# Moving x's turned 32 x 32 squares through memory instead of 16 DMAs a batch

## The chip, the cores and the metric

The kernel runs on one core of a Trainium2 chip. What counts is the device time of one execution in microseconds. TensorE does the products, VectorE (DVE) and ScalarE (ACT) the element-wise work, GpSimd (POOL) the gathers of rows by index and some element-wise work; SyncE (SP) issues every other DMA. Each engine works through its own instructions in order and waits on semaphores.

## The reference, cut to what matters

A gated linear attention makes x, a mixture of experts sends each token to 2 of 8 experts, and a bilinear layer ends it.

```
state = alpha[t][:, None] * state + outer(k[t], v[t]);  y[t] = q[t] @ state    # 4 x 8 heads, 768 steps, 48 wide
x = y as 3072 tokens x 384 features
noisy = x @ w_gate + log1p(exp(x @ w_noise)) * noise;  top2, softmax over the two
out[mask] += weight * (relu(x[mask] @ w1[e]) @ w2[e])                          # w1: 384 x 1024, w2: 1024 x 384
result = ((x @ w_a) * (x @ w_b)) @ w_out                                       # on the experts' output; 384 x 1536
```

All is float32. The kernel splits each operand of a product into a high and a low part of TensorE's fast float32 kind and adds three products (`prod3`, L785 to L787).

## The kernel before, in words

**Stages.** The first 151 us hold the attention and the router. Then come the experts 0 to 7, up to 832 rows each, and from about 641 us the third stage: six blocks of 512 tokens, each in twelve steps (one per 128 of the 1536 hidden features), an up unit (L1100) and a down unit (L1119) per step. An expert has eight up units (`up_unit`, two halves of 384 rows), a tail of up to 64 more rows that runs in a branch, and six down units (`down_unit`, 128 rows each, 24 products) with a down tail.

**How x gets its layout.** A product contracts over features, so the gathered rows (128 tokens x 384 features) have to be turned: features onto partitions, in three groups `k` of 128. For expert 0, expert 1 and the first block of the third stage TensorE transposes them (`transposed`, L485). For experts 2 to 7, and the other five blocks, DVE turns each 32 x 32 square in place (`blocks`, L504), which leaves the squares in the wrong partitions of `tb`; then `turn` (L506) moves them: for each of 4 x 4 partition pairs one DMA from `tb` to `raw`, in runs of 32 floats, for a batch of up to four row tiles. `parted` (L515) copies a piece of `raw` as the high part on ACT (L517) and takes the low part on DVE (L518). An expert's seven tiles make two batches, of four tiles and of three.

**Order.** The order of instructions is written out by hand. While expert e multiplies, expert e+1 is prepared: its rows are gathered in up units 0 to 6 (L477), turned two units later; the first batch is moved after up unit 6 (L1051), the second after the tail's products (L1059), both by SP. Before down unit j, piece j of the next x is split (L1061). After a down unit ACT evicts the bank into an output tile `o` (L876; the pool `outs` has 3 buffers) and SP stores it to `y2` (L877). Down units use two PSUM banks in turn, so unit j+2 needs the eviction of unit j.

SP also loads the experts' weights (`w_load`, L113, into 6 staging tiles), split by ACT and POOL (L108, L109); and it feeds `decode` (L928): the third stage's weights come as 64-bit numbers, 36 chunks of 384 KB (`wd`, L931), are turned into float32 by ACT (L937, L938, L945), DVE (L939, L942, L943, L949) and POOL (L946, L947), and stored to memory again (`w3f`, L950). `bg` moves a chunk one step per up or down unit; a chunk's first work on ACT stands two `bg` calls behind the issue of its DMA.

In the third stage the next block's x is gathered from `y2` in steps 1 to 4, summed and turned in steps 3 to 6, moved in step 7 (L1142) and split, a tile each, in steps 9 to 12 (L1144).

Of the kernel before, what the change touches and what calls it, by code (L numbers as in the profile page):

```python
# [7 lines left out]
F32 = mybir.dt.float32  # L8
# [13 lines left out]
DM = H * D  # L22
KD = DM // 128
E = 8
# [32 lines left out]
def moe_kernel(ctx: ExitStack, tc, qka, afirst, v, wgn, noise, w1, w2, w3, out):  # L57
# [15 lines left out]
    total = base_of(E - 1) + CAP  # L73
    early = base_of(E - 1) + CAPL
    y2 = tc.dram_tile([total, DM], F32, name="y2")
    wide = w3.dtype != F32
    w3f = tc.dram_tile([128, 3 * NF2 * 384], F32, name="w3f") if wide else None

# [402 lines left out]
    def transposed(t, m, h, l, pt=None):  # L481

        pt = pt or trbank()
        for k in range(KD):
            nc.tensor.transpose(pt[:, k * 128:k * 128 + m], t[:m, k * 128:k * 128 + 128], ident[:m, :m])  # L485
        ptv = pt[:, :DM].rearrange("p (k n) -> p k n", k=KD)[:, :, :m]
        nc.scalar.activation(h, ptv, AF.Copy)
        nc.vector.tensor_tensor(l, ptv, h.bitcast(F32), op=ALU.subtract)
# [5 lines left out]


    flips = {}

    def blocks(key, j, t, m):

        b = j // 4  # L500
        if j % 4 == 0:
            flips[key, b] = tl(tp, [128, 12, 128], F32, "tb", bufs=2)
        tb = flips[key, b][:, 3 * (j % 4):3 * (j % 4) + 3]
        nc.vector.transpose(tb[:m].rearrange("p k n -> p (k n)"), t[:m])  # L504

    def turn(key, b, raw, sizes):  # L506

        tb = flips.pop((key, b))
        for ti in range(4):
            n = 3 * sum(m > 32 * ti for m in sizes)  # L510
            for c in range(4):
                nc.sync.dma_start(raw[32 * c:32 * c + 32, 12 * b:12 * b + n, 32 * ti:32 * ti + 32],  # L512
                                  tb[32 * ti:32 * ti + 32, :n, 32 * c:32 * c + 32])

    def parted(src, h, l):  # L515
# [4 lines left out]
    raws_of = {}  # L520
    sizes = [min(128, CAP - 128 * j) for j in range(NJ)]

    def x_blocks(e, j):
        blocks(e, j, gat.pop((e, j)), sizes[j])

    def x_turn(e, b):
        if b == 0:
            raws_of[e] = tl(tp, [128, 3 * NJ, 128], F32, "raw")
        turn(e, b, raws_of[e], sizes[4 * b:4 * b + 4])

    def x_part(e, j):
        s = slice(128 * j, 128 * j + sizes[j])
        parted(raws_of[e][:, 3 * j:3 * j + 3, :sizes[j]], Xh[:, :, s], Xl[:, :, s])

    def routing(s):
        yield from choose(s)
# [240 lines left out]
    HB = tl(hpool, [128, 2 * NF1 * ROWS], F32R, "HB")  # L777
    Hh = HB[:, :NF1 * ROWS].rearrange("p (f n) -> p f n", f=NF1)
    Hl = HB[:, NF1 * ROWS:].rearrange("p (f n) -> p f n", f=NF1)
    outs = sctx.enter_context(tc.tile_pool(name="outs", bufs=3))  # L780

    def prod3(ps, a, b, first, last):

# [206 lines left out]
    def x2_blocks(i):  # L990
        blocks("x2", i % TB, x2r.pop(i)[1], 128)

    def x2_turn():
        raws_of["x2"] = tl(tp, [128, 3 * NJ, 128], F32, "raw")
        turn("x2", 0, raws_of["x2"], [128] * TB)

    def x2_part(i):
        j = i % TB
        parted(raws_of["x2"][:, 3 * j:3 * j + 3], *x2_at(i))


    more_rows = {}
# [36 lines left out]
    for e in range(1, E - 1):  # L1039
        for f in range(NF1):  # L1040
            up_unit(e, f, [(0, MAIN // 2), (MAIN // 2, MAIN // 2)])
            if f == 2:
                load_more_rows(e)
            if e == 2 and f == 5:
                over = nc.values_load(flag[0:1, 0:1], min_val=0, max_val=1)
            if f < NJ:
                gather(e + 1, f)
            if f >= 2:
                x_blocks(e + 1, f - 2)
            if f == 6:  # L1050
                x_turn(e + 1, 0)  # L1051
            w_split()
            w_load()
            bg()
        tail = up_tail(e)
        next(tail)
        bg()
        x_blocks(e + 1, 6)
        x_turn(e + 1, 1)  # L1059
        for j in range(NJ):  # L1060
            x_part(e + 1, j)  # L1061
            if j < NJ - 1:
# [82 lines left out]

    for u in range(NB * NF2):
        blk, f = divmod(u, NF2)
# [13 lines left out]
    with tc.tile_pool(name="over", bufs=1) as op:  # L1161
# [10 lines left out]
        with tc.If(over > 0):  # L1172
# [11 lines left out]
            def flip(dst, src):  # L1184
                pt = bank(0)
                for k in range(KD):
                    ks = slice(k * 128, k * 128 + 128)
                    nc.tensor.transpose(pt[:, ks], src[:, ks], ident)
# [86 lines left out]
```

## Time and profile before

| | us |
|---|---|
| median of the timed runs (lowest, highest) | 1103.93 (1101.8, 1105.57) |
| the profiled execution's own time | 1101.91 |
| its span, first to last instruction | 1100.1 |
| TensorE busy | 1036.3 (94%) |
| VectorE, ScalarE, GpSimd busy | 510.7, 416.7, 414.3 |
| mean granted clock of TensorE | 0.973 |

Busy time says how long an engine had an instruction in work. A wait is the idle time of an engine just before an instruction, put down to whatever released it. The chain of work that ended last is followed back from the end, at each step to what released it. The granted clock is TensorE's, as a share of 2.4 GHz. SP's instructions, which issue DMAs, are its queue's (SPq) and not counted as busy.

### The profile page before, as it was taken

The page shows a single profiled execution, that of the slowest core. Times are in us where ns is not written, and L with a number is a line of the kernel's source. Part 1 is how long each engine was busy: PE and PEld are TensorE (multiplying, and loading weights), DVE is VectorE, ACT ScalarE, POOL GpSimd, SP SyncE. Part 2 cuts the span into 40 slices and gives each one's busy share as a digit, 9 for nine tenths or more (in the row PEclk, how much of TensorE's full clock was granted, in tenths as well). Part 3 has the DMA queues.
Part 4 walks back from the last instruction along what each step waited for, and adds up shares of the span by engine and source line. Part 5 has one row for each costly group of instructions (what it writes and reads, how often), then busy time and mean ns, then how long its engine had stood idle before and what let it go on. Part 6 is the DMA issues. An engine that isn't in the chain of part 4 may idle for free.

```text
span 1100.1 us, 18122 instructions
## 1 busy us (share of the span) xinstructions
PE 1036.3 (94%) x6868; PEld 953.2 (87%) x6868; DVE 510.7 (46%) x940; ACT 416.7 (38%) x913; POOL 414.3 (38%) x446
## 2 busy tenths in 40 slices
PE   7998879999989999979989899999999999999997
PEld 5887779999989989879979888888888888888886
DVE  8998575663725545545534335323233232232221
ACT  2554322644526455434444424322222222222222
POOL 5688414573827465655744532411020020000000
PEclk9999779999999999998999999999999999999998
DMA  8776114556556666655663633313012021010000
GB/s 326 262 287 234 40 35 134 157 155 176 171 116 203 128 221 141 208 147 165 177 174 100 193 112 73 101 51 65 18 53 46 29 64 24 29 26 4 29 1 31
DMA packets 154511, 129.47 MB, mean 118 GB/s; under 512 B 102832, under 2 KB 138416, under 8 KB 154416
## 3 DMA queue, kind: packets, MB, share of 16 engines
q1 hardware_dynamic: 147888, 108.54, 34.0%
q0 software_dynamic: 6528, 19.67, 6.1%
q8 instruction: 58, 0.95, 0.4%
q14 instruction: 37, 0.30, 0.1%
HBM read 89.83 MB, written 26.74 MB: 106 GB/s over the span
## 4 chain that ended last, share of the span: by engine, by line
PE 65%; SPq 9%; DVE 8%; DMA 5%; POOL 3%; issue 3%; ACT 2%; ACTq 0%; DVEq 0%; POOLq 0%
PE bank L786 20%; PE bank L787 20%; PE bank L785 20%; SPq L512 8%; DMA wd<-w 3%; DMA y<-o 2%; DVE pm L641 1%; POOL W L109 1%; DVE D L606 1%; DVE A L610 1%; POOL row L477 1%; SPq L113 1%; PE bank L652 1%; PE bank L636 1%; DMA wst<-w3f 1%
## 5 line engine op out<-in xcount | busy, mean ns | idle before, releaser
L109 POOL TENSOR_TENSOR W<-wst,W 128x384 fp32r<-128x384 f32 x136 | 143.3, 1058 | 169.9 <-ACT W L108 168.3
L785 PE MATMUL bank<-W,HB 128*128 128x384 f32 x528 | 182.2, 345 | 18.6 <-ACT o L876 18.6
L787 PE MATMUL bank<-W,HB 128*128 128x384 f32 x528 | 179.4, 340 | 0.0
L786 PE MATMUL bank<-W,HB 128*128 128x384 f32 x528 | 179.2, 339 | 0.0
L785 PE MATMUL bank<-X,W 128*128 128x384 f32 (+1 forms) x483 | 170.7, 353 | 5.7 <-ACT X L517 5.7
L786 PE MATMUL bank<-X,W 128*128 128x384 f32 (+1 forms) x483 | 170.1, 352 | 0.3 <-DVE X L518 0.2
L1112 DVE TENSOR_TENSOR p<-bank,a 128x512 f32<-128x512 f32 x72 | 49.8, 692 | 258.9 <-PE bank L787 254.8
L787 PE MATMUL bank<-X,W 128*128 128x384 f32 (+1 forms) x483 | 169.9, 352 | 0.0
L785 PEld LDWEIGHTS bank<-W,HB 128*128 128x128 f32 x528 | 101.0, 191 | 23.7 <-ACT o L876 21.8
L972 POOL DMA_INDIRECT row<-y,row x48 | 46.6, 970 | 188.5 <-DVE row L980 172.0
L1114 ACT ACTIVATE HB<-p 128x512 fp32r<-128x512 f32 x72 | 45.5, 632 | 155.8 <-DVE p L1112 153.6
L1110 ACT ACTIVATE a<-bank 128x512 f32<-128x512 f32 x72 | 43.0, 597 | 160.7 <-PE bank L787 160.7
L786 PEld LDWEIGHTS bank<-W,HB 128*128 128x128 f32 x528 | 101.0, 191 | 1.7
L785 PEld LDWEIGHTS bank<-X,W 128*128 128x128 f32 x483 | 92.9, 192 | 10.2 <-ACT X L517 6.3
L787 PEld LDWEIGHTS bank<-W,HB 128*128 128x128 f32 x528 | 100.9, 191 | 0.0
L786 PEld LDWEIGHTS bank<-X,W 128*128 128x128 f32 x483 | 92.9, 192 | 4.7 <-DVE X L518 0.8
L803 DVE SCALAR_TENSOR_TENSOR HB<-bank,HB 128x384 fp32r<-128x384 f32 x128 | 69.3, 553 | 57.8 <-ACT HB L802 50.2
L787 PEld LDWEIGHTS bank<-X,W 128*128 128x128 f32 x483 | 92.7, 192 | 3.9
L802 ACT ACTIVATE HB<-bank 128x384 fp32r<-128x384 f32 x128 | 62.0, 490 | 82.0 <-PE bank L787 76.3
L477 POOL DMA_INDIRECT row<-xd,idx x56 | 60.5, 1081 | 39.9 <-DVE idx L386 23.2
L108 ACT ACTIVATE W<-wst 128x384 fp32r<-128x384 f32 x144 | 72.9, 519 | 2.8 <-DMA wst<-w3f 2.4
L1115 DVE TENSOR_TENSOR HB<-p,HB 128x512 fp32r<-128x512 f32 x72 | 49.9, 692 | 50.3 <-ACT HB L1114 48.9
(262 smaller groups left out, 1946.5 us busy)
## 6 DMA issues: line engine op xcount, KB each, us to landing
wst<-w SPq DMA_DIRECT2D x128, 192.0 KB
ring<-qka SPq DMA_DIRECT2D x22, 768.0 KB
wd<-w SPq DMA_DIRECT2D x36, 384.0 KB
y<-o SPq DMA_DIRECT2D x48, 192.0 KB
raw<-tb SPq DMA_DIRECT2D x176, 48.0 KB
w3f<-u SPq DMA_DIRECT2D x36, 192.0 KB
wst<-w3f SPq DMA_DIRECT2D x36, 192.0 KB
v<-v SPq DMA_DIRECT2D x12, 384.0 KB
```

The source lines that it names most:

```text
L108: nc.scalar.activation(h, raw, AF.Copy)
L109: eng.tensor_tensor(l, raw, h.bitcast(F32), op=ALU.subtract)
L477: nc.gpsimd.indirect_dma_start(out=t[:m], out_offset=None, in_=xd[:SPLIT * 128] if a else xd, in_offset=bass.IndirectOffsetOnAxis(ap=ix, a ...
L512: nc.sync.dma_start(raw[32 * c:32 * c + 32, 12 * b:12 * b + n, 32 * ti:32 * ti + 32], tb[32 * ti:32 * ti + 32, :n, 32 * c:32 * c + 32])
L785: nc.tensor.matmul(ps, ah, bh, start=first, stop=False)
L786: nc.tensor.matmul(ps, ah, bl, start=False, stop=False)
L787: nc.tensor.matmul(ps, al, bh, start=False, stop=last)
L802: nc.scalar.activation(Hh[:, f, s], pu, AF.Relu)
L803: nc.vector.scalar_tensor_tensor(Hl[:, f, s], pu, 0.0, Hh[:, f, s].bitcast(F32), op0=ALU.max, op1=ALU.subtract)
L972: nc.gpsimd.indirect_dma_start(out=t, out_offset=None, in_=src, in_offset=bass.IndirectOffsetOnAxis(ap=row[:, i, k:k + 1], axis=0))
L1112: nc.vector.tensor_tensor(p, ps[1], a, op=ALU.mult)
L1115: nc.vector.tensor_tensor(l, p, h.bitcast(F32), op=ALU.subtract)
```

## The change

The squares go through a scratch tensor `xt` in memory: one DMA (two for the second batch) writes `tb` out row by row, four read it back, each for 32 partitions and in runs of 96 floats. For that, DVE's turning reads every third feature and writes the three groups side by side, and feature 3r + k now lies in group k; TensorE's transposes read with the same step, and the host lays out the rows of `w1`, `w_a` and `w_b` to match. In the expert stages the reading back stands one unit behind the writing out (up unit 7; before down unit 1), in the third stage one step behind (step 8). The third stage splits two tiles each in steps 10 and 11. The pool `outs` gets a fourth buffer.

```diff
+    xt = tc.dram_tile([ROWS, DM], F32, name="xt")
-            nc.tensor.transpose(pt[:, k * 128:k * 128 + m], t[:m, k * 128:k * 128 + 128], ident[:m, :m])
+            nc.tensor.transpose(pt[:, k * 128:k * 128 + m], t[:m, k::KD], ident[:m, :m])
...
-        nc.vector.transpose(tb[:m].rearrange("p k n -> p (k n)"), t[:m])
+        nc.vector.transpose(tb[:m].rearrange("p (c k n) -> p c k n", c=4, k=KD),
+                            t[:m].rearrange("p (c r k) -> p c k r", c=4, k=KD))
-    def turn(key, b, raw, sizes):
+    def turn_out(key, b, rows):
         tb = flips.pop((key, b))
-        for ti in range(4):
-            n = 3 * sum(m > 32 * ti for m in sizes)
-            for c in range(4):
-                nc.sync.dma_start(raw[32 * c:32 * c + 32, 12 * b:12 * b + n, 32 * ti:32 * ti + 32],
-                                  tb[32 * ti:32 * ti + 32, :n, 32 * c:32 * c + 32])
+        n, m = divmod(rows, 128)
+        d = xt[512 * b:512 * b + 128 * n].rearrange("(j p) d -> p j d", p=128)
+        nc.sync.dma_start(d, tb[:, :n])
+        if m:
+            nc.sync.dma_start(xt[512 * b + 128 * n:512 * b + rows], tb[:m, n])
+    def turn_in(raw, b, rows):
+        for c in range(4):
+            nc.sync.dma_start(raw[32 * c:32 * c + 32, 16 * b:16 * b + rows // 32],
+                              xt[512 * b:512 * b + rows, 96 * c:96 * c + 96].rearrange("(n r) w -> r n w", r=32))
-    def parted(src, h, l):
+    def parted(raw, m, h, l):
+        src = raw[:, :m // 32].rearrange("p t (k n) -> p k t n", k=KD)
+        h, l = (x.rearrange("p k (t n) -> p k t n", n=32) for x in (h, l))
...
-    outs = sctx.enter_context(tc.tile_pool(name="outs", bufs=3))
+    outs = sctx.enter_context(tc.tile_pool(name="outs", bufs=4))
...
             if f == 6:
-                x_turn(e + 1, 0)
+                x_out(e + 1, 0)
+            if f == 7:
+                x_in(e + 1, 0)
...
-        x_turn(e + 1, 1)
         for j in range(NJ):
+            if j == 0:
+                x_out(e + 1, 1)
+            if j == 1:
+                x_in(e + 1, 1)
             x_part(e + 1, j)
...
         if f == 6:
-            x2_turn()
-        if f >= 12 - TB:
-            x2_part(i + f - 12 + TB)
+            turn_out("x2", 0, BLK)
+        if f == 7:
+            new_raw("x2")
+            turn_in(raws_of["x2"], 0, BLK)
+        if f in (9, 10):
+            for j in range(2):
+                x2_part(i + 2 * (f - 9) + j)
```

## Rows read from the trace of the kernel before

**Rows 1.** The page, chain that ended last: shares of the span by line.

```profile
PE bank L786 20%; PE bank L787 20%; PE bank L785 20%; SPq L512 8%; DMA wd<-w 3%; DMA y<-o 2%; DVE pm L641 1%; POOL W L109 1%; DVE D L606 1%; DVE A L610 1%; POOL row L477 1%; SPq L113 1%; PE bank L652 1%; PE bank L636 1%; DMA wst<-w3f 1%
```

**Rows 2.** Waits of TensorE: who, for whom, us in total, times, longest.

```profile
PE bank L785 <- ACT o L876: 18.6, 10, 5.9
...
PE bank L785 <- ACT X L517: 5.7, 2, 3.7
...
PE bank L858 <- ACT o L876: 2.4, 1, 2.4
```

**Rows 3.** Timeline of SP: start, us, line, DMA, count.

```profile
296.70 11.60 SPq L512 DMA_DIRECT2D raw<-tb  x16
...
309.00 0.43 SPq L931 DMA_DIRECT2D wd<-w  x1
```

**Rows 4.** Timeline of ACT; in brackets the idle time before and its end.

```profile
313.27 0.56 ACT L937 ACTIVATE ah<-wd 128x384 f32<-128x384 f32 x1 [9.36 <-DMA wd<-w]
...
374.76 0.52 ACT L517 ACTIVATE X<-raw 128x384 fp32r<-128x384 f32 x1 [7.01 <-DMA raw<-tb]
```

**Rows 5.** Windows at half clock: us, busy by engine, PEclk, DMA share, GB/s.

```profile
633.77:637.18 3.41, 3.41 (x14) 3.31 (x14) 0.78 (x2) 1.24 (x3) 0.00 (x0) 0.50 0.00 1
sum 22.94, PE 22.94 PEld 22.84 DVE 15.35 ACT 14.72 POOL 16.74; mean PE 3.82 PEld 3.81 DVE 2.56 ACT 2.45 POOL 2.79
```

**Rows 6.** Timeline of TensorE, inside a half-clock stretch and outside one.

```profile
317.16 0.52 PE L785 MATMUL bank<-W,HB 128*128 128x384 f32 x1
317.48 0.52 PE L786 MATMUL bank<-W,HB 128*128 128x384 f32 x1
...
372.79 0.33 PE L785 MATMUL bank<-W,HB 128*128 128x384 f32 x1
...
373.66 0.34 PE L787 MATMUL bank<-W,HB 128*128 128x384 f32 x1
```

**Rows 7.** Line 512: duration of an issue in ns, min/median/max, first and last start.

```profile
L512 SPq DMA_DIRECT2D raw<-tb x272: 585/618/1939, 234.0 to 989.5; - x136
```

**Rows 8.** The chain in order of time: pieces that are a y DMA.

```profile
385.56 2.04 DMA y<-o
...
507.10 3.46 DMA y<-o
...
566.05 7.23 DMA y<-o
```

**Rows 9.** DMA packets, MB, share: 752 to 764 us (L512), 1091 to 1098 (outputs).

```profile
q1 hardware_dynamic: 6000, 0.74, 43.0%
...
q1 hardware_dynamic: 576, 0.79, 30.9%
```

**Rows 10.** Timelines of SP and TensorE: first L512, first down product, two experts.

```profile
234.04 11.23 SPq L512 DMA_DIRECT2D raw<-tb  x16
...
242.08 0.33 PE L785 MATMUL bank<-W,HB 128*128 128x384 f32 x1
...
476.64 4.58 SPq L512 DMA_DIRECT2D raw<-tb  x5
...
480.08 0.34 PE L785 MATMUL bank<-W,HB 128*128 128x384 f32 x1
```

**Rows 11.** Timeline of ACT, the last eviction.

```profile
1094.49 0.49 ACT L1129 ACTIVATE o<-bank 128x384 f32<-128x384 f32 x1 [1.93 <-DMA out<-o]
```

**Rows 12.** Timeline of TensorE, first products of a block of the third stage.

```profile
713.43 0.49 PE L785 MATMUL bank<-HB,EX 128*128 128x512 f32 x1
...
714.53 0.40 PE L787 MATMUL bank<-HB,EX 128*128 128x512 f32 x1
...
715.46 0.39 PE L785 MATMUL bank<-HB,EX 128*128 128x512 f32 x1
```

**Rows 13.** Groups by line and shape, DVE: busy us, mean ns, idle before.

```profile
L504 DVE STREAM_TRANSPOSE tb<-row 128x384 f32<-128x384 f32 x56 | 32.1, 572 | 3.4 <-DMA row<-xd,idx 2.5
```

**Rows 14.** Line 485, weight load: ns min/median/max, first and last start, forms.

```profile
L485 PEld LDWEIGHTS bank<-ident,row x54: 136/141/231, 141.9 to 635.8; 128*128 128x128 f32 x48, 64*128 64x128 f32 x6
```

More of the change, by code (lines that the diff above doesn't have):

```diff
@@ L496, in moe_kernel @@
     flips = {}
+    raws_of = {}
+    sizes = [min(128, CAP - 128 * j) for j in range(NJ)]
     def blocks(key, j, t, m):
-        b = j // 4
         if j % 4 == 0:
-            flips[key, b] = tl(tp, [128, 12, 128], F32, "tb", bufs=2)
-        tb = flips[key, b][:, 3 * (j % 4):3 * (j % 4) + 3]
-        nc.vector.transpose(tb[:m].rearrange("p k n -> p (k n)"), t[:m])
-    def turn(key, b, raw, sizes):
-        tb = flips.pop((key, b))
-        for ti in range(4):
-            n = 3 * sum(m > 32 * ti for m in sizes)
-            for c in range(4):
-                nc.sync.dma_start(raw[32 * c:32 * c + 32, 12 * b:12 * b + n, 32 * ti:32 * ti + 32],
-                                  tb[32 * ti:32 * ti + 32, :n, 32 * c:32 * c + 32])
@@ L515, in parted @@
-    def parted(src, h, l):
+            flips[key, j // 4] = tl(tp, [128, 4, DM], F32, "tb", bufs=2)
+        tb = flips[key, j // 4][:, j % 4]
+        nc.vector.transpose(tb[:m].rearrange("p (c k n) -> p c k n", c=4, k=KD),
+                            t[:m].rearrange("p (c r k) -> p c k r", c=4, k=KD))
+    def turn_out(key, b, rows):
+        tb = flips.pop((key, b))
+        n, m = divmod(rows, 128)
[3 more added lines that the diff above has]
+            nc.sync.dma_start(xt[512 * b + 128 * n:512 * b + rows], tb[:m, n])
@@ L517, in parted @@
+    def turn_in(raw, b, rows):
[5 more added lines that the diff above has]
+        h, l = (x.rearrange("p k (t n) -> p k t n", n=32) for x in (h, l))
         nc.scalar.activation(h, src, AF.Copy)
         nc.vector.tensor_tensor(l, src, h.bitcast(F32), op=ALU.subtract)
-    raws_of = {}
@@ L521, in moe_kernel, with new_raw, x_out, x_in @@
-    sizes = [min(128, CAP - 128 * j) for j in range(NJ)]
+    def new_raw(key):
+        raws_of[key] = tl(tp, [128, 4 * NJ, 96], F32, "raw")
     def x_blocks(e, j):
         blocks(e, j, gat.pop((e, j)), sizes[j])
-    def x_turn(e, b):
+    def x_out(e, b):
+        turn_out(e, b, sum(sizes[4 * b:4 * b + 4]))
+    def x_in(e, b):
         if b == 0:
-            raws_of[e] = tl(tp, [128, 3 * NJ, 128], F32, "raw")
-        turn(e, b, raws_of[e], sizes[4 * b:4 * b + 4])
+            new_raw(e)
+        turn_in(raws_of[e], b, sum(sizes[4 * b:4 * b + 4]))
@@ L531, in x_part @@
     def x_part(e, j):
         s = slice(128 * j, 128 * j + sizes[j])
-        parted(raws_of[e][:, 3 * j:3 * j + 3, :sizes[j]], Xh[:, :, s], Xl[:, :, s])
+        parted(raws_of[e][:, 4 * j:4 * j + 4], sizes[j], Xh[:, :, s], Xl[:, :, s])
     def routing(s):
@@ L991, in x2_blocks @@
         blocks("x2", i % TB, x2r.pop(i)[1], 128)
-    def x2_turn():
-        raws_of["x2"] = tl(tp, [128, 3 * NJ, 128], F32, "raw")
-        turn("x2", 0, raws_of["x2"], [128] * TB)
     def x2_part(i):
         j = i % TB
-        parted(raws_of["x2"][:, 3 * j:3 * j + 3], *x2_at(i))
+        parted(raws_of["x2"][:, 4 * j:4 * j + 4], 128, *x2_at(i))
     more_rows = {}
@@ L1187, in flip @@
                     ks = slice(k * 128, k * 128 + 128)
-                    nc.tensor.transpose(pt[:, ks], src[:, ks], ident)
+                    nc.tensor.transpose(pt[:, ks], src[:, k::KD], ident)
                 nc.scalar.activation(dst, pt[:, :DM], AF.Copy)
@@ L1257 @@
         "noise": inputs["moe_noise"].reshape(NT, 128, E).transpose(1, 0, 2),
-        "w1": inputs["moe_w1"].reshape(E, KD, 128, NF1, 128).transpose(0, 2, 3, 1, 4).reshape(E, 128, NF1, 384),
+        "w1": inputs["moe_w1"].reshape(E, 128, KD, NF1, 128).transpose(0, 1, 3, 2, 4).reshape(E, 128, NF1, 384),
         "w2": inputs["moe_w2"].reshape(E, NF1, 128, DM).transpose(0, 2, 1, 3),
-        "w3": np.stack([inputs[k].reshape(KD, 128, NF2, 128).transpose(1, 2, 0, 3).reshape(128, NF2, 384)
+        "w3": np.stack([inputs[k].reshape(128, KD, NF2, 128).transpose(0, 2, 1, 3).reshape(128, NF2, 384)
                         for k in ("moe2_w_a", "moe2_w_b")]
```

## Prediction

> **What bounds the kernel now.** I began with the chain that ended last. Three lines of TensorE's products hold 20% of the span each, and behind them stands one that is no arithmetic: SP's queue at L512, 8% [rows 1]. L512 issues the DMAs that move the turned squares of x from `tb` to `raw`. A share of a chain is no loss, because TensorE may work meanwhile, so I read next what TensorE itself waits for. It waits 18.6 + 2.4 us for ACT's eviction `o` (L876) and 5.7 us for ACT's copy of x (L517), 26.7 us together [rows 2].
>
> Why ACT is late stands in the timelines. One batch of turned squares is 16 DMAs and holds SP for 11.60 us; only then does SP issue the encoded third-stage weights (`wd`), at 309.00 [rows 3]. ACT comes to L937 with no weights to read and idles 9.36 us until 313.27; in the next expert, until 374.76, it idles 7.01 us for the squares themselves [rows 4]. All engines run in order, so one late DMA holds every ACT instruction behind it, `o` among them, and TensorE runs out of free banks. Ten of the eleven stalls on `o`, and both on L517, lie between 276 and 580 us, where experts 2 to 6 prepare the next expert's x in this way; one lies in expert 1.
>
> The stalls cost more than their length. Behind the five longest, in which TensorE stood for 2 to 5.9 us, the granted clock is 0.50 for a while, the 1.2 GHz level: six such stretches sum to 22.94 us, of which one of 3.41 us, at 633.77, belongs to another wait (that for L488) [rows 5]; that leaves 19.53 us. There products start 0.32 us apart, against 0.174 us (five steps in 0.87) at full clock [rows 6], so 1 - 0.174/0.32 = 0.46 of it is lost: 8.9 us.
>
> **The change part by part.**
>
> *Fewer issues on SP.* An issue at L512 takes 0.618 us [rows 7], 0.66 us with the pause behind it, 16 of them 10.6 us. The new batch is one write to memory (two for the second batch of an expert, whose last 64 rows go alone) and four reads back. With the 0.66 us of a like-formed issue that is 3.3 to 4.0 us, some 7 us of SP saved per batch, 14 per expert, in just the stretch that makes `wd` and `y` late. If all waits of ACT go, the stalls of 26.7 us and the slow clock behind them, 8.9 us, go with them: 35.6 us.
>
> *The round trip.* The four reads wait on SP until the write has landed. A `y` DMA of 192 KB lands 2.04 to 7.23 us after its issue, 3.46 in a usual case [rows 8]. Four output DMAs (768 KB, all in 1536-byte runs) hold 0.309 x 16 engines x 7 us = 34.6 us of engine time, 2.2 us over 16 engines [rows 9]; one of them 0.54. So the write of 768 KB lands after 3.7 to 8.9 us, 5.1 usual (the `y` figure plus 3 x 0.54). The fourth read is issued 3 x 0.66 = 2.0 us later and lands 2.0 to 7.2 us after that, 3.5 usual. The whole: 7.7 to 18.1 us, and I take 10.6. The data itself is no worse than now: 6000 runs of 128 bytes cost 0.43 x 16 x 12 = 82.6 us of engine time, 13.8 ns each [rows 9], 5.2 us per batch over 16 engines; 2048 runs of 384 bytes lie between the 2.2 us of long runs and those 5.2 us (3.0 by a line between the two sizes), to which the write adds its 2.2.
>
> *What this wait may hold.* The first piece of x is split ahead of the eviction of down unit 0, and TensorE needs that bank when down unit 1 ends. In the tightest expert the squares are ready at 476.64 and the down units start at 480.08 [rows 10]; two units are 48 products of 0.174 = 8.35 us; less 1.0 us for the copy (0.52, [rows 4]) and an eviction of like size, 10.8 us are left. In expert 1 the same sum gives 15.4 us (squares at 234.04, down units from 242.08); the other four lie between. So the usual 10.6 us just fits and I count no stall; at 18.1 us the excess is 2.7 to 7.3 us, a mean of 5, six times 30 us, with six slow stretches of 3.41 x 0.46 = 1.57 us, 39 us in all. Queued on SP behind the wait are a load of expert weights, the next `wd` or `w3f`, the second batch's write and `y` of unit 0. At the usual landing SP stands some 5 us less what passes between the two steps, against 11.6 us now. The second batch is read back after `y` of unit 0 and needed after three more down units, 12.5 us, so it is hidden; uncovered, its excess would fall on ACT at unit 4.
>
> *Fourth output buffer.* In the expert stages it lets `o` run one more unit ahead of a late `y`; its gain is inside the 26.7. At the end ACT idles 1.93 us before the last output because the third-last buffer is still in flight [rows 11]. With four that wait goes and the last DMA leaves 1.9 us sooner: 1.9 us, all on the path. The same waits at other block ends hold no TensorE.
>
> *Third-stage x one step earlier.* Now the fourth piece is split in step 12, and the next block's second product waits for it: the first two products take 1.10 us, from 713.43 to 714.53, where the next four take 0.93, 0.23 each [rows 12]. Steps 10 and 11 with two pieces each end that: 1.10 - 0.47 = 0.63 us at each of five block ends, 3.2 us. Two pieces in a step add 1 us to ACT and to DVE in a step of 6.2 us. The round trip lies in two steps with SP idle.
>
> *Permuted features.* The squares and 54 TensorE transposes now read every third element. No row shows a three-element step, so I bound it: from nothing to doubling. DVE's transpose is 0.572 us [rows 13], off the path; doubled it takes 0.6 us from the 10.8. TensorE's weight load for one is 141 ns [rows 14]; doubled and not hidden, 54 x 0.141 = 7.6 us. A gain is excluded, since the same elements are read. I take nothing, as the count of elements stays, and the rows show nothing else that would set it. The transposes of the overflow branch don't run here.
>
> The Trainium skill ("SBUF — State Buffer", section "Door 1: The DMA port swizzle") speaks against this part: SBUF is read in lines of 16 bytes, and reads that touch a line fewer than twice lose speed; a 12-byte step hits a line 1.3 times. No row here shows it. What it would make of the time is the third rival below.
>
> *Sum.* 35.6 + 1.9 + 3.2 = 40.7 us. I hold back 4 us: 2 for a round trip that is late in one or two experts, 2 for `wd`, which takes 4.3 us from issue (309.00) to ACT's release (313.27) even when SP is free [rows 3, 4]. That leaves 36.7. The profiled execution took 1101.9 us (span 1100.1 plus 1.8 around it), 2.0 below the median of the timed runs, 1103.9; by the median the forecast is 1103.9 - 36.7 = 1067.2, about 1067 us.
>
> **The rivals.**
>
> 1. *Half the stalls stay, because `wd` is the cause and not SP.* For: ACT waits for `wd` in the largest stall [rows 4], and 4.3 us of its delay is the transfer. Against: only 4.3 of the 9.36 us there pass after its issue, the other 5.1 before it. Half of 35.6, 18, stays, of which 2 are held back already: 1067 + 16 = 1083 us.
>
> 2. *Slower.* The wait for the write's landing takes the place of the issues: SP stands at step 7 in each of six experts, with `wd` and `y` behind it, and ACT stands at the first piece of x. It decides where the round trip passes 18 us in the mean expert: there the new stalls (39 us) eat the 40.7 won. At 20 us the excess is 6.9 us on average, six times 41.4 + 9.4 = 50.8, less 40.7: 1104 + 10 = 1114 us. For: the slowest `y` took 7.23 us [rows 8]. Against: it needs that everywhere, and twice in a row.
>
> 3. *The strided reads cost.* TensorE's 54 transposes pay 7.6 us: 1067 + 7.6 = 1075 us, a little more if the DVE delay uncovers the round trip. For: nothing in the trace; against: nothing either.
>
> 4. *The change does nothing where it aims:* another wait stands just behind each stall and only the last stage's 5.1 us come: 1099 us. Against: L512 stands ahead of the late DMA [rows 3].
>
> **How the numbers follow.** Forecast 0.70, rival 1 0.12, rival 3 0.08, rival 2 0.05, rival 4 0.05. All of the first three are faster by over 0.3% (3.3 us, about what a measurement here can tell from no change), and most of rival 4: 0.92 faster, 0.03 no change, 0.05 slower. The forecast's own range is from 1058 (nothing held back, and 5 us more should the stall before 633.77 and its slow stretch go too) to 1076. To leave out no more than 2 in 10 it must reach rival 1, so 1058 to 1086.
>
> **What would show it.** L512's 16 issues per batch gone from SP and the issue of `wd` right behind the write; TensorE's waits for L876 and L517 below 4 us together; granted clock 1.00 between 276 and 580 us except for single stretches; block ends with 0.23 us between the first two products; the last eviction right behind the third. Each reading back within 11 us of the write's issue would show the round trip as sized. It is wrong if ACT idles for `raw` in most experts (round trip too long), if ACT still idles for `wd` by 5 us or more (rival 1), or if TensorE's transposes lie further apart (rival 3).

## The result and the profile after

The changed kernel takes 1064.16 us (median of 4 runs, 1062.98 to 1065.93); the kernel before took 1104.75 us beside it (1101.8 to 1105.68). The ratio is 0.9638, with a 95% interval from 0.9614 to 0.9662: 40.6 us less by the medians, where 36.7 were forecast. The profiled execution of the changed kernel is its slowest run, 1065.93 us (span 1064.2), 36.0 less than that of before; the sums below are made between these two profiled executions. One run further down, 1264.71 us of the kernel with features in order at a granted clock of 0.746, is left out of that kernel's median and ratio.

Most lines have moved by some 14: the products of `prod3` are L799 to L801, ACT's eviction `o` L890, its copy of x L528, the first work on `wd` L951; the write to `xt` is L514 (L516 for 64 rows), the reading back L521.

| stretch, us | before | after | difference |
|---|---|---|---|
| start to the first down product of expert 1 | 242.08 | 244.63 | +2.55 |
| from there to the first down product of expert 7 | 361.89 | 325.13 | -36.76 |
| from there to the first eviction of the last block | 487.03 | 485.70 | -1.33 |
| from there to the end of the span | 9.15 | 8.70 | -0.45 |

The first line is no effect of the change: across the runs of all kernels below that point comes between 240.7 and 244.6 us. What counts most is the second line, the six experts in whose time an x is turned for the next one.

The chain that ended last in the kernel after, shares of the span by line:

```profile
PE bank L799 25%; PE bank L800 25%; PE bank L801 25%; DMA raw<-xt 2%; DVE pm L655 1%; DMA xt<-tb 1%; DVE D L620 1%; DVE A L624 1%; PE bank L650 1%; PE bank L666 1%; PE bank L486 1%; SPq L521 0%; POOL row L986 0%; POOL row L478 0%; POOL W L110 0%
```

Against [rows 1] SP's queue has gone from 8% to nothing, and TensorE's products have grown from 60% to 75%: the chain now runs through arithmetic. `wd` and `y` are not in it any more; the new round trip (`xt<-tb`, `raw<-xt`) is, with 3%.

Waits of TensorE in the kernel after (who, for whom, us in total, times, longest), the two lines that concern the experts and what follows them:

```profile
PE bank L486 <- DVE X L489: 4.6, 1, 4.6
...
PE bank L799 <- ACT o L890: 1.6, 3, 0.6
```

Of the 26.7 us of [rows 2], 1.6 are left on `o` (2.9 in a second profiled execution of the same kernel), and no line for the copy of x is left. The first line is a wait that the change was not about; it was there before and is taken up below.

Windows over the same work, six experts from the first down product of expert 1 to that of expert 7, first of the kernel before and then of the kernel after (window: us, busy by engine, granted clock, DMA share, GB/s):

```profile
242.08:603.97 361.89, 334.88 (x1846) 327.29 (x1844) 178.01 (x300) 170.71 (x386) 204.43 (x192) 0.97 0.60 163
```

```profile
244.63:569.76 325.13, 322.67 (x1845) 318.58 (x1844) 179.18 (x300) 171.70 (x386) 200.95 (x193) 1.00 0.68 202
```

The same count of products, to one record. What TensorE did not work fell from 361.89 - 334.88 = 27.0 us to 2.5, and the time in which it worked fell by 12.2 us, with the granted clock up from 0.97 to 1.00 of 2.4 GHz. 24.5 + 12.2 = 36.7 us is the whole of the second line of the table.

Two more windows of the kernel after, from 276 us up to the fall of the clock during that wait for DVE, and the stretch at half clock:

```profile
276.00:598.70 322.70, 316.97 (x1813) 312.56 (x1812) 179.49 (x293) 171.24 (x385) 205.43 (x197) 1.00 0.68 203
598.73:605.56 6.83, 5.57 (x20) 5.48 (x21) 3.34 (x7) 2.56 (x6) 0.29 (x1) 0.50 0.13 45
```

The six half-clock stretches of [rows 5] are gone but the one behind the wait for DVE, and that one is twice as long as before, 6.83 against 3.41 us. The length is one of this execution: in the second one of the same kernel the stretch is as long as before:

```profile
601.09:604.50 3.41, 3.41 (x14) 3.31 (x13) 1.17 (x3) 1.65 (x5) 0.00 (x0) 0.50 0.00 0
```

SP's timeline in the kernel after, in the same expert as [rows 3] (start, us, line, DMA, count):

```profile
297.55 0.43 SPq L514 DMA_DIRECT2D xt<-tb  x1
...
298.66 0.53 SPq L945 DMA_DIRECT2D wd<-w  x1
302.82 1.92 SPq L521 DMA_DIRECT2D raw<-xt  x4
304.83 0.43 SPq L114 DMA_DIRECT2D wst<-w  x1
305.31 0.43 SPq L964 DMA_DIRECT2D w3f<-u  x1
305.79 0.43 SPq L514 DMA_DIRECT2D xt<-tb  x1
306.32 0.51 SPq L516 DMA_DIRECT2D xt<-tb  x1
```

Where 16 issues held SP for 11.60 us, the write takes 0.43 us, and `wd` leaves 1.1 us behind its start instead of 12.3 us. SP then stands for 3.6 us until the write has landed (a load of weights, `w3f` and the second batch's write are queued behind it) and issues the four reads in 1.92 us.

ACT's timeline in the same stretch (in brackets the idle time before and what ended it):

```profile
304.64 0.56 ACT L951 ACTIVATE ah<-wd 128x384 f32<-128x384 f32 x1
...
310.59 0.53 ACT L528 ACTIVATE X<-raw 128x384 fp32r<-128x384 f32 x1 [4.95 <-DMA raw<-xt]
311.02 0.47 ACT L890 ACTIVATE o<-bank 128x384 f32<-128x384 f32 x1
```

ACT finds `wd` there, without the 9.36 us of [rows 4]. It still idles before x, 4.95 us here, and the eviction stands behind that; but it does so while TensorE has two banks to fill. That the idle time of ACT has not gone and TensorE's has is what its waits for DMAs say:

```profile
ACT X L528 <- DMA raw<-xt: 25.7, 6, 5.8
...
ACT ah L951 <- DMA wd<-w: 6.3, 7, 2.1
```

Before, ACT waited 71.2 us for `wd` (17 times), 21.4 for the squares and 19.5 for `y`; `y` has no line any more.

### The profile page after: what moved, and what is told of

Read it like the earlier page. It is cut to its first block, busy times and chain, and to the rows that moved or that the text cites. A ratio compares the mean times of both kernels' runs of the same rounds, so it can differ in the third digit from the quotient of the medians.

```text
span 1064.2 us, 17897 instructions
## 1 busy us (share of the span) xinstructions
PE 1028.1 (97%) x6868; PEld 950.8 (89%) x6868; DVE 518.3 (49%) x940; ACT 417.9 (39%) x913; POOL 410.9 (39%) x446
## 4 chain that ended last, share of the span: by engine, by line
PE 79%; DVE 6%; DMA 3%; POOL 2%; issue 2%; ACT 1%; SPq 0%; POOLq 0%; ACTq 0%; DVEq 0%
PE bank L799 25%; PE bank L800 25%; PE bank L801 25%; DMA raw<-xt 2%; DVE pm L655 1%; DMA xt<-tb 1%; DVE D L620 1%; DVE A L624 1%; PE bank L650 1%; PE bank L666 1%; PE bank L486 1%; SPq L521 0%; POOL row L986 0%; POOL row L478 0%; POOL W L110 0%
## 5 line engine op out<-in xcount | busy, mean ns | idle before, releaser
L110 POOL TENSOR_TENSOR W<-wst,W 128x384 fp32r<-128x384 f32 x136 | 140.3, 1037 | 138.7 <-ACT W L109 137.1
L799 PE MATMUL bank<-W,HB 128*128 128x384 f32 x528 | 179.9, 341 | 1.6 <-ACT o L890 1.6
L801 PE MATMUL bank<-W,HB 128*128 128x384 f32 x528 | 177.8, 337 | 0.0
L800 PE MATMUL bank<-W,HB 128*128 128x384 f32 x528 | 177.6, 336 | 0.0
L799 PE MATMUL bank<-X,W 128*128 128x384 f32 (+1 forms) x483 | 168.7, 349 | 0.8 <-DVE HB L817 0.8
L800 PE MATMUL bank<-X,W 128*128 128x384 f32 (+1 forms) x483 | 168.1, 348 | 0.0
L801 PE MATMUL bank<-X,W 128*128 128x384 f32 (+1 forms) x483 | 167.9, 348 | 0.0
L799 PEld LDWEIGHTS bank<-W,HB 128*128 128x128 f32 x528 | 100.0, 189 | 4.3 <-ACT o L890 2.6
L800 PEld LDWEIGHTS bank<-W,HB 128*128 128x128 f32 x528 | 99.9, 189 | 1.7
L801 PEld LDWEIGHTS bank<-W,HB 128*128 128x128 f32 x528 | 99.7, 189 | 0.0
L799 PEld LDWEIGHTS bank<-X,W 128*128 128x128 f32 x483 | 91.4, 189 | 5.0 <-DVE HB L817 1.3
L801 PEld LDWEIGHTS bank<-X,W 128*128 128x128 f32 x483 | 91.4, 189 | 3.9
L800 PEld LDWEIGHTS bank<-X,W 128*128 128x128 f32 x483 | 91.4, 189 | 3.9 <-issue 0.3
```

The lines of the kernel that those rows point to most:

```text
L110: eng.tensor_tensor(l, raw, h.bitcast(F32), op=ALU.subtract)
L799: nc.tensor.matmul(ps, ah, bh, start=first, stop=False)
L800: nc.tensor.matmul(ps, ah, bl, start=False, stop=False)
L801: nc.tensor.matmul(ps, al, bh, start=False, stop=last)
```

## The experiments

The theory: SP's queue of 16 issues per batch was the cause, through the DMAs that stood behind it, and the round trip just fits. The rivals: the bytes per run or `wd` by itself; the buffer; the strided reads, as a cost that makes the gain smaller. The first four ran together, against 1102.32 us of the kernel before (11 runs). The changed kernel itself ran in this group only; between groups the ratios to the kernel before are what compares.

**The changed kernel again.**

> The changed kernel itself, as the mark for the three beside it. Theory (SP's issues made the encoded weights and the y stores late, and ACT and TensorE with them): 1062 to 1066 us again, ratio 0.962 to 0.966. No rival says otherwise.

1062.52 us (1060.48 to 1065.5), ratio 0.9629 [0.9607, 0.9652]. What the next three are held against.

**Three output buffers.**

```diff
-    outs = sctx.enter_context(tc.tile_pool(name="outs", bufs=4))
+    outs = sctx.enter_context(tc.tile_pool(name="outs", bufs=3))
```

> The changed kernel with three output buffers again. Theory: with SP free a y store lands about 3.5 us after its issue, so three buffers do in the expert stages; only the end pays, where the last eviction waits 1.9 us again: 1.9 us slower than the changed kernel (range 1 to 4), TensorE's wait for the eviction below 4 us. Rival (the fourth buffer is what cured the stalls): TensorE's wait for the eviction returns to 10 to 20 us and the time goes up by 12 to 25 us.

1063.24 us, 0.9645 [0.9624, 0.9667]: 0.7 us more, and the intervals overlap. In the experts the fourth buffer does nothing: the waits on `o` are 1.4 us (2 times) with three. At the end the wait of [rows 11] is back, as ACT's timeline of this kernel shows:

```profile
1051.36 1.53 ACT L1144 ACTIVATE o<-bank 128x384 f32<-128x384 f32 x3 [1.25 <-PE bank L801]
1054.65 0.49 ACT L1144 ACTIVATE o<-bank 128x384 f32<-128x384 f32 x1 [1.77 <-DMA out<-o]
```

The last eviction starts 3.29 us after the first; with four buffers it is 1.6 us. And yet from the first eviction to the end it is 8.98 us here against 8.70. Of the 1.9 us that I had put on the path, 1.3 still show at the last output's issue, 2.50 us after the first eviction with four buffers and 3.81 with three; they are lost behind it (see the last experiment).

**The third stage's split as before.**

```diff
-        if f in (9, 10):
-            for j in range(2):
-                x2_part(i + 2 * (f - 9) + j)
+        if f >= 12 - TB:
+            x2_part(i + f - 12 + TB)
```

> The changed kernel with the third stage's split back in steps 9 to 12, one tile each. Theory: 0.63 us at each of five block ends, 3.2 us slower than the changed kernel (range 2.5 to 3.8), the first two products of a block taking 1.10 us again. Rival (the first product's wait was hidden by what follows): 0 to 1 us.

1065.61 us, 0.9673 [0.965, 0.9696]: 3.1 us more, as expected (the two intervals just touch, 0.965 and 0.9652). TensorE's timeline at the first products of a block in this kernel, and below it in the kernel after:

```profile
677.64 0.48 PE L799 MATMUL bank<-HB,EX 128*128 128x512 f32 x1
678.41 0.50 PE L800 MATMUL bank<-HB,EX 128*128 128x512 f32 x1 [0.29 <-DVE HB L529]
678.74 0.39 PE L801 MATMUL bank<-HB,EX 128*128 128x512 f32 x1
```

```profile
681.09 0.39 PE L799 MATMUL bank<-HB,EX 128*128 128x512 f32 x1
681.32 0.40 PE L800 MATMUL bank<-HB,EX 128*128 128x512 f32 x1
681.55 0.40 PE L801 MATMUL bank<-HB,EX 128*128 128x512 f32 x1
```

The first two products take 1.10 us, to the hundredth what [rows 12] have, against 0.46. The wait in brackets is 0.29 us; the rest of the loss lies in products that run alone, so that counting idle time only would have given less than half.

**Features in order.** The round trip stays; DVE's turning and TensorE's transposes read adjoining features again, and the host's layouts are those of before.

```diff
-            nc.tensor.transpose(pt[:, k * 128:k * 128 + m], t[:m, k::KD], ident[:m, :m])
+            nc.tensor.transpose(pt[:, k * 128:k * 128 + m], t[:m, k * 128:k * 128 + 128], ident[:m, :m])
...
-                            t[:m].rearrange("p (c r k) -> p c k r", c=4, k=KD))
+                            t[:m].rearrange("p (k c r) -> p c k r", c=4, k=KD))
...
```

> The changed kernel without the permuted features: group k is again features 128k to 128k+127, the transposes on TensorE read contiguous columns, and DVE reads its squares as runs of 32 floats in another order, so that the squares still leave as 96-float runs. The changed kernel's trace shows a TensorE weight load of 202 ns for a transpose where the kernel before has 141, and 696 ns for a DVE transpose where it has 572. Theory (the three-element step costs what these rows say): back to 141 and 572 ns, and 54 x 0.061 = 3.3 us faster at most, range 1.5 to 3.5, nearly all before 250 us. Rival (the weight loads are covered, and the later start of the experts is chance): within 1 us of the changed kernel.

1062.28 us (5 runs), 0.9635 [0.9612, 0.9659]. No difference to the kernel with the stride that the times can show (0.2 us, with intervals of some 2.5 us to either side), though the instructions themselves differ. TensorE's weight loads of the transposes (ns min/median/max), strided in the kernel after and then in order:

```profile
L486 PEld LDWEIGHTS bank<-ident,row x54: 185/202/283, 144.5 to 602.8; 128*128 128x128 f32 x48, 64*128 64x128 f32 x6
```

```profile
L486 PEld LDWEIGHTS bank<-ident,row x54: 135/141/230, 142.2 to 601.2; 128*128 128x128 f32 x48, 64*128 64x128 f32 x6
```

And DVE's turning of squares (busy us, mean ns of one, idle before), in the same order:

```profile
L506 DVE STREAM_TRANSPOSE tb<-row 128x384 f32<-128x384 f32 x56 | 39.0, 696 | 4.9 <-DMA row<-xd,idx 4.1
```

```profile
L506 DVE STREAM_TRANSPOSE tb<-row 128x384 f32<-128x384 f32 x56 | 32.1, 573 | 4.7 <-DMA row<-xd,idx 3.9
```

The stride costs 61 ns per weight load (43%) and 123 ns per turning (21%). In order they are as in [rows 13, 14]. 54 x 0.061 = 3.3 us of weight loading and 6.9 us of DVE lie beside other work, for all that the times show. The rule of the Trainium skill that I had weighed ("SBUF — State Buffer", section "Door 1: The DMA port swizzle") agrees with these rows in its direction: reads at a 12-byte step are slower. What it would have made of this kernel's time, the third rival, did not come.

The next four ran together, against 1101.64 us of the kernel before (13 runs).

**The reading back later.** It is issued before down unit 0's x instead of after up unit 7, with the tail's products between; the write stays where it is.

```diff
-            if f == 7:
-                x_in(e + 1, 0)
...
             if j == 0:
+                x_in(e + 1, 0)
                 x_out(e + 1, 1)
```

> The changed kernel with the first batch of an expert read back only after the tail's products, just ahead of the second batch's write, 2 to 3.5 us later than now. Theory (the first piece of x has to arrive by the end of down unit 1, and the changed kernel only just keeps that: the piece is split 0.9 to 1.0 us past my limit in three experts, with 0.5 to 0.6 us of stall): stalls of TensorE on the eviction grow by 2 to 3.5 us in each of five or six experts, 10 to 20 us, and half-clock stretches of 3.41 us come back behind those of 2 us and more, 1.6 us each: 12 to 28 us slower than the changed kernel, 1076 to 1092 us. Rival (the place has slack; what counted was only that SP is free): within 3 us of the changed kernel.

1081.22 us (1077.93 to 1083.7), 0.9818 [0.9782, 0.9854]: 18.7 us more than the changed kernel's 1062.52 (some 21 by the ratios), with the intervals far apart. The same transfers, the first read issued 5.9 to 8.9 us behind the write instead of 4.8 to 5.6, and half of the gain is gone. TensorE's wait for `o` in this kernel, and then ACT's timeline at its longest wait for the squares:

```profile
PE bank L799 <- ACT o L890: 13.6, 4, 4.6
```

```profile
533.02 0.52 ACT L528 ACTIVATE X<-raw 128x384 fp32r<-128x384 f32 x1 [9.91 <-DMA raw<-xt]
```

So the round trip is on the edge. This is the mechanism of rival 2 at work, and it shows that it was the place of the two steps that kept it away.

**Sixteen reads.** Each of the four reads is cut into row tiles of 128; the runs stay 384 bytes, the bytes are the same, SP issues 16 again (12 for the second batch).

```diff
-            nc.sync.dma_start(raw[32 * c:32 * c + 32, 16 * b:16 * b + rows // 32],
-                              xt[512 * b:512 * b + rows, 96 * c:96 * c + 96].rearrange("(n r) w -> r n w", r=32))
+            for r0 in range(0, rows, 128):
+                m = min(128, rows - r0)
+                q = 16 * b + r0 // 32
+                nc.sync.dma_start(raw[32 * c:32 * c + 32, q:q + m // 32],
+                                  xt[512 * b + r0:512 * b + r0 + m, 96 * c:96 * c + 96]
+                                  .rearrange("(n r) w -> r n w", r=32))
```

> The changed kernel with each batch read back by 16 DMAs of 48 KB (12 and less in the second batch) in place of 4, the same bytes in the same runs of 384 bytes. Theory (the number of issues is what holds SP): an issue takes 0.48 us, so twelve more hold SP 5.8 us longer per batch, the first piece of x comes 4 to 6 us later, the encoded weights and y stores behind it too: 24 to 42 us slower than the changed kernel, 1088 to 1106 us, much of the way back. Rival (the 128-byte runs, not the issues, made the batch slow): the runs are still 384 bytes, so within 4 us of the changed kernel.

1081.44 us (1080.28 to 1083.43), 0.9819 [0.9783, 0.9854]: 18.9 us more than the changed kernel; the mechanism as expected, the size below it. An issue takes a median of 430 ns here (248 of them), not the 618 ns of [rows 7]. SP's timeline, TensorE's waits and ACT's waits in this kernel:

```profile
300.67 9.05 SPq L524 DMA_DIRECT2D raw<-xt  x16
```

```profile
PE bank L803 <- ACT X L532: 6.8, 2, 4.4
...
PE bank L803 <- ACT o L894: 6.6, 5, 2.3
```

```profile
ACT ah L955 <- DMA wd<-w: 47.9, 19, 7.9
```

SP is held for 9.05 us, ACT waits for `wd` again, 47.9 us in all, and TensorE waits at the two places of [rows 2]. The size of the runs is what it is in the changed kernel; only the number of DMAs, and with it their size, differs. That is the theory's own test, and it holds for the half of the gain that it takes back. A kernel with few issues in runs of 128 bytes was not built, so what part of the other half the run length has stays open.

**The kernel before with four buffers.**

```diff
-    outs = sctx.enter_context(tc.tile_pool(name="outs", bufs=3))
+    outs = sctx.enter_context(tc.tile_pool(name="outs", bufs=4))
```

> The kernel before with a fourth output buffer and nothing else. Theory: ACT's waits for a y store (19.5 us in four) mostly stand beside waits for the encoded weights and for the squares that stay; 1.9 us come at the end and 0 to 4 us in the experts: 1098 to 1102 us, ratio 0.994 to 0.998. Rival (late buffers are the cause of the stalls): 15 to 25 us faster, 1080 to 1089 us.

1103.60 us (10 runs, 1100.4 to 1104.85), 1.0008 [0.999, 1.0026]: nothing, a miss for me. TensorE's and ACT's waits in this kernel:

```profile
PE bank L785 <- ACT o L876: 20.3, 7, 5.7
```

```profile
ACT ah L937 <- DMA wd<-w: 79.9, 17, 10.5
```

ACT's 19.5 us for `y` are gone, its wait for `wd` has grown by 8.7 us, and TensorE waits as before. A wait that goes uncovers the next one in the same engine's order when both have one cause. And at the end, where ACT's wait of 1.93 us went too, no gain came.

**The kernel before with `wd` loaded one step earlier.** One more step between issue and use, and a third buffer for it; the squares still go in 16 DMAs.

```diff
-        wd = tl(dec, [128, 384, 2], I32, "wd", bufs=2)
+        wd = tl(dec, [128, 384, 2], I32, "wd", bufs=3)
         nc.sync.dma_start(wd.rearrange("p n o -> p (n o)"), w3[:, c].bitcast(I32))
         yield
+        yield
```

> The kernel before with the encoded weights' first work one unit later behind the issue of their DMA (three calls instead of two, and a third buffer for them): the 16 issues stay on SP, only ACT no longer meets the late weights. Theory (SP's issues delay both the encoded weights and the squares, and the weights come first in most stalls): a unit is 4.2 us in the down phase, so waits of 5 to 11 us shrink by that; the stalls behind them fall from 26.7 to 8 to 14 us and half of the half-clock stretches go: 15 to 24 us faster, 1080 to 1090 us. Rival (the weights' wait only hides the wait for the squares and y behind it): 0 to 6 us faster. The other rival (the weights alone are the cause): 35 us faster, 1069 us.

1082.26 us (1081.44 to 1082.91), 0.9822 [0.9788, 0.9856]: 19.4 us less than before, half of the gain, with nothing of the change in it. Waits of TensorE and of ACT in this kernel:

```profile
PE bank L785 <- ACT o L876: 11.2, 7, 3.1
```

```profile
ACT X L517 <- DMA raw<-tb: 33.0, 6, 8.0
ACT o L876 <- DMA y<-o: 31.3, 8, 7.0
...
ACT ah L938 <- DMA wd<-w: 18.8, 8, 4.1
```

So half of the harm of SP's queue went through `wd`; with that out of the way the other half shows, through `y` and the squares themselves (19.5 and 21.4 us before, 31.3 and 33.0 now). Rival 1 had the right path, but not its end: `wd` was late because of SP, for with four reads ACT's wait for it falls to 6.3 us at the old distance.

The last three ran against 1103.08 us of the kernel before (11 runs). Two tried to remove the stall of 4.6 us and the half clock behind it, at expert 7's last transposes.

**Features in order, and all gathers of the third stage's first x in unit 2.**

```diff
...
-        for q in {2: (0, 1), 3: (2, 3)}.get(j, ()):
+        for q in {2: (0, 1, 2, 3)}.get(j, ()):
...
```

> The kernel with plain groups, and all eight gathers for the third stage's first block issued before down unit 2 of the last expert, not four there and four before unit 3. It is aimed at the largest stall left: TensorE stands 4.5 us before a transpose (L486) at 598 us and then runs 6.8 us at half clock, 3.1 us lost. ACT gets there late, since it waits 1.29 and 1.39 us for third-stage weights and 0.79 us for the last gathered row. Theory (GpSimd's splits keep weights from loading, the gathers only add to it): the row comes some 2 us earlier but the splits go behind the gathers, 0 to 3 us faster than with plain groups. Rival (the gathers are the cause): 5 to 7 us faster.

1062.78 us, 0.9628 [0.9599, 0.9656]. No gain; the stall is 5.7 us. The gathers are not what is late.

**The same, and the split of the third stage's weights on DVE alone, none on GpSimd.**

```diff
...
-            split(w3c.pop(0), *w3_part(*divmod(done[0], 3)), nc.vector if done[0] % 2 else nc.gpsimd)
+            split(w3c.pop(0), *w3_part(*divmod(done[0], 3)), nc.vector)
...
```

> As plain_gather, and the low parts of the third stage's weights all taken on DVE, none on GpSimd, which is busy with the gathers. DVE idles some 3 us per down unit there. Theory (GpSimd holds back both the weights and the rows): ACT's waits for weights and rows before 598 us go, the stall of 4.5 us falls under 2 us and the 6.8 us at half clock with it: 4 to 7 us faster than the changed kernel, 1055 to 1060 us. Rival (DVE's splits now delay the sums and the transposes' low parts instead): within 2 us.

1061.33 us (1058.29 to 1063.35), 0.9616 [0.9585, 0.9647]. The stall is 3.3 us, and the half clock behind it 3.41 instead of 6.83 us; but the time can't be told from the changed kernel's, and 3.41 us is also what that kernel's second profiled execution has. A miss by size: the time is the rival's. Why the stall stands there is not settled. Two rows of the kernel after, DVE's and GpSimd's timelines ahead of it, look like an answer:

```profile
595.18 3.22 DVE L110 TENSOR_TENSOR W<-wst,W 128x384 fp32r<-128x384 f32 x1 [3.45 <-issue]
```

```profile
595.08 2.90 POOL L110 TENSOR_TENSOR W<-wst,W 128x384 fp32r<-128x384 f32 x3
```

One subtraction on DVE takes 3.22 us while GpSimd does three of the same form beside it; in the kernel without GpSimd's the timeline has the same instruction at 0.56 us. DVE's ends at 598.40, 0.42 us after GpSimd's last. The Trainium skill ("SBUF — State Buffer", section "SBUF: two separate sides") has a rule of this form: a DVE operation with two inputs in SBUF and a GpSimd operation that reads SBUF exclude each other, and the one that comes second stands still until the first is done; the two rows agree with it, 3.22 us against 2.90 + 0.56 less the 0.10 us by which GpSimd started sooner. But this is not what makes the stall. In the second profiled execution of the same kernel the subtraction starts 0.80 us ahead of GpSimd's three and has its usual length,

```profile
594.87 0.56 DVE L110 TENSOR_TENSOR W<-wst,W 128x384 fp32r<-128x384 f32 x1 [2.55 <-DMA wst<-w3f]
```

and the stall is 4.17 us all the same. Over all the profiled kernels, with the change and without it, the stall is 3.3 to 5.7 us (4.61 in the kernel before with four buffers), so the 0.9 us between before and after say nothing of the change. What makes the stall stays open.

**The branch for tokens beyond the experts' capacity left out.** It stands at the end of the program and does not run with these inputs.

```diff
-    with tc.tile_pool(name="over", bufs=1) as op:
...
-        with tc.If(over > 0):
...
```

> The changed kernel without the branch for overfull experts, which these inputs never enter (left out: that branch alone). In the changed kernel a 16 KB packet of the instruction queue (q8, 1.77 us on one DMA engine) starts 0.2 us after the last output DMA's first packets, and that DMA ends 2.3 us behind its median packet; span from the first last-block eviction to the end is 8.7 to 9.0 us with three and with four buffers. Theory (the packet loads code that lies behind the third stage, and holds the last output on its engine): without the branch the packet goes, and that stretch falls by 1.5 to 2.5 us, to 6.2 to 7.5 us. Rival (the output's landing is slow by itself): 8.5 to 9 us as before.

1058.11 us (1057.74 to 1059.61), 0.9585 [0.9548, 0.9623]. From the first of the last four evictions to the end it is 5.03 us, where the kernel before has 9.15, after 8.70, and after with three buffers 8.98. DMA queues in the last microseconds (packets, MB, share of 16 engines) in the kernel after, 1055.4 to 1062, and in this one, 1052 to 1057.8:

```profile
q8 instruction: 2, 0.03, 2.6%
q14 instruction: 4, 0.03, 1.9%
```

```profile
q1 hardware_dynamic: 576, 0.79, 36.3%
...
out<-o SPq DMA_DIRECT2D x4, 192.0 KB, 1.9
```

Two queues that fetch instructions are gone; the outputs land 1.9 us after their issue. The stretch falls by 3.7 us, where 1.5 to 2.5 were expected from the packet on the DMA engine, and most of it is something else. SP's rows on the line of the branch (duration in ns min/median/max, first and last start), in the kernel after and then with three buffers:

```profile
L1191 SPq EVENT_SEMAPHORE  x8: 17/17/17, 1061.2 to 1062.5; - x8
...
L1191 SPq COMPARE_BRANCH  x1: 53/53/53, 1058.4 to 1058.4; - x1
```

```profile
L1191 SPq EVENT_SEMAPHORE  x8: 17/17/17, 1058.1 to 1058.7; - x8
...
L1191 SPq COMPARE_BRANCH  x1: 53/53/53, 1055.6 to 1055.6; - x1
```

Behind its branch SP does nothing for 2.7 us in the kernel after and for 2.5 us with three buffers and in the kernel before (1095.4 to 1097.9). Then it goes through eight waits on semaphores, among them those for the last outputs, and the program ends some 1.7 us later. With three buffers and in the kernel before, the last output has landed (1058.16 and 1097.65 us) when SP comes to the wait for it, and costs nothing. With four buffers SP reaches the branch 1.2 to 1.4 us sooner, the output lands at 1062.32 us in the kernel after, and SP waits 0.8 us for it. There the trace shows a packet of q8, 16 KB, that takes 1.77 us up to 1060.90 us; the last eight packets of that output start only as it ends. So most of the 3.7 us is SP's stand behind the branch, and the late landing is where most of the fourth buffer's gain went. That SP stands for code is likely, since packets of q8 and q14 run in that time in all three traces, but no run shows it apart from the branch. This kernel has the lowest time of all, but it leaves out what inputs that overflow would need.

## Why the prediction was right, and where its terms were off

*The cause: right.* SP's 16 issues delay `wd`, `y` and the squares, ACT stands for them, TensorE for ACT. Taking the issues away took 25.1 of 26.7 us of TensorE's waits; putting 16 back at the new size of runs returned half of the loss; more distance for `wd` alone takes half of it from the kernel before.

*The size of it: 35.6 forecast, 36.8 measured.* The idle part was 24.5 us, the part in which TensorE works 12.2, for which I had 8.9 by the half-clock stretches. An estimate for most of the 3.3 us between: at a stall the last product before it runs alone, 0.33 us instead of the 0.174 us of [rows 6], 0.16 us at each of 13 stalls, 2.1 us. The same is seen at the block ends.

*The total: near, in part by luck.* The terms came to 40.7 us before 4 us were held back; the stretches from expert 1 on give 38.5 (36.76 + 1.33 + 0.45), and the later start of the one profiled execution takes 2.55 of them. What was held back for a late round trip and for `wd` covered what the fourth buffer and the stall before the transposes took instead.

*The round trip: mis-sized, at little cost.* I took 10.6 us of a range from 7.7 to 18.1. From the write's issue to the first copy of x on ACT it is 11.7, 13.0, 12.5, 13.0, 12.2 and 11.9 us in the six experts. ACT idles for `raw` in all six, which the prediction had named as a sign of being wrong; what it costs is TensorE's wait behind it, and that is small. The first half was right: the reads leave 4.75 to 5.6 us after the write, 5.1 forecast. Their issue is cheaper than I took, as the row of that line in the kernel after shows:

```profile
L521 SPq DMA_DIRECT2D raw<-xt x68: 302/478/1540, 241.5 to 949.1; - x68
```

The four leave 0.53 us apart in the shown expert and not 0.66, with 0.478 us for the issue instead of 0.618. The failed term is the landing of the last read, 3.5 us in the sum, 4.9 to 6.7 us from its issue to ACT's copy in the six experts: from 304.25 to 310.59 in the one shown. The DMA queues in that stretch, 297.5 to 312 us of the kernel after:

```profile
q1 hardware_dynamic: 3706, 3.24, 79.2%
```

I had taken the landing of a `y` DMA in 1536-byte runs as the nearest row and counted the data in a term of its own that I never added; with the engines 79% busy the two probably add up, which no run shows by itself. What held was the budget: by the same sum, made with the times of the kernel after, experts 3 to 5 are late by 0.9 to 1.0 us each, and TensorE waits there 0.50, 0.50 and 0.61 us, the 1.6 us of its line for `o`. The 2 us held back for this were the right size; the 2 for `wd` were not needed, as its 6.3 us of waits on ACT reach TensorE nowhere.

*The fourth buffer: the step that failed.* 1.9 us forecast at the end; 0.2 to 0.3 us by that stretch (9.15 to 8.95 us in the kernel before, 8.98 to 8.70 in the changed one), 0.7 us at most by the medians. ACT's wait went, as I had it. That it stood on the path was wrong: with three buffers the end hangs on SP's stand behind the branch and not on the last output, and with four the last output lands 6.9 us after the first eviction, no sooner than with three (6.7 and 6.8), and becomes what SP waits for.

*The third stage: 3.2 forecast, 3.1 measured.* It is not seen whole in the table's third line, because the stall before the transposes (3.69 us before, 4.56 after) and the work of TensorE at half clock behind it (3.41, now 5.57 us of the 6.83; 46% of the difference is 1.0 us) took about 1.9 us back: 3.1 - 1.9 = 1.2 of the 1.33 us there. I had priced that stall at no change or a gain; it differs from execution to execution. In the second one, with 4.17 and 3.41 us, the third line is 484.39 us, 2.64 less than before, as 3.1 less 0.5 would have it.

*The strided reads: right as a sum, by luck in the price.* I took nothing because nothing in the rows spoke for a cost. There is one, 43% and 21% per instruction, which lies beside other work. Rival 3's price would have been 3.3 us, not 7.6, had it been on the path.

*By the medians* the gain is 40.6 us and by the profiled executions 36.0; 2.6 us of this is the later start in that one run, the rest is in the spread of the runs (1060.5 to 1065.9 in nine runs of the changed kernel).

## What to carry to other kernels

Read a wait back to the in-order queue that issued the late DMA, and count what stands ahead of it there: here 10 or 11 fewer issues a batch (5 or 6 instead of 16) were worth 37 us, though the data now goes out to memory and back. Before placing a trip through memory, price its landing with the DMA engines as busy as they are in that stretch, and check the place, not only the length: the same reads issued 1 to 4 us later cost 18.7 us. And before adding a buffer ask what else stands between its DMA and the end: here a branch that SP takes 2.5 us to leave.

## What the runs showed of the hardware that was not expected

- A three-element step makes a weight load of a transpose take 202 ns instead of 141, and a DVE turning of 128 x 384 take 696 instead of 573.
- An issue of a DMA with 32 partitions and 384-byte runs takes 430 to 478 ns on SP; with 128-byte runs, in [rows 7], 618.
- Behind a branch whose body does not run SP stood for 1.3 to 3.0 us in the twelve traced kernels that have it, 2.7 in the kernel after; from the first of the last four evictions to the end it is 7.17 to 9.15 us in them, 5.03 without the branch.
- A 16 KB packet of an instruction queue took 1.77 us, and the last eight packets of the last output started only as it ended.
- A DVE subtraction of 0.56 us took 3.22 us beside three of GpSimd's that had started 0.10 us ahead of it, and 0.56 us where it started 0.80 us ahead of them.
